# Attention and a gated MLP in one kernel: the bias load of the last 64 rows of two heads, as one load or as one per head

## The chip, the cores and the metric

One core of a Trainium2 chip runs the whole program. The metric is the device time of one execution, in microseconds (us). The kernel before takes 776.21 us, the median of 3 runs (774.19 to 776.37).

## The reference

What is computed, cut to what matters here. There are 4 batches, 8 heads, 576 positions and 64 columns per head. The bias depends on head and positions alone, so it is the same for every batch.

```
scores = scale * q @ k.T                        # per batch and head, 576 x 576
x      = log1p(|i - j|) / log1p(max(i, 1))
bias   = relu(x * w1 + b1) @ w2                 # 576 x 576 x 8 heads
attn   = softmax(scores + bias)
y      = attn @ v                               # 2304 tokens x 512
h      = y @ w_in                               # 512 -> 2048
out    = (max(h, 0) + alpha * min(h, 0)) @ w_out
```

## The kernel before

The bias is computed once. Every `bias_tile` makes it for 16 rows and all heads and writes it to a scratch tensor in HBM (L495); the scratch has three blocks of 256, 256 and 64 rows, each laid out row, head, column. So one row of one head is 576 floats, 2304 bytes in one piece, and the next row of the same head lies 8 heads further on.

The attention is cut into units, one for each batch, half of the heads (`hf`), pair of heads in it (`pr`) and range of rows (`rng`). A unit with `rng` 0 has rows 0 to 255, in two groups of 128 rows. A unit with `rng` 1 has rows 256 to 575: two groups of 128 rows, and then a last group of 64 rows in which the two heads of the pair share one tile, head 0 in partitions 0 to 63 and head 1 in partitions 64 to 127. There are 32 units, 16 of them with `rng` 1, so 16 such last groups.

For each group of a unit:

- SyncE (SP) issues the load of the bias into tile `fg`. A group of 128 rows has one load of 576 KB (L739), in which each partition gets two neighbouring heads, 4608 bytes in one piece. The last group has one load of 288 KB (L751), 128 rows of 2304 bytes.
- TensorE (PE) computes the scores in PSUM (L585 in float32 for the first batch, L586 in float16 parts for the others).
- VectorE (DVE) adds bias and scores and takes the row maximum in one instruction (L765), over `fg` in place.
- ScalarE (ACT) takes the exponential (L768); the sums are turned into a factor (L771, L773, L775).
- Then the rows are normalised and transposed. In most units GpSimd (POOL) scales (L790), PE transposes (L799), and ACT or DVE copies the result out of PSUM (L809, L810). In the units of batch 1 half 1, batch 2 and batch 3 half 1, POOL or ACT writes a float16 part into a tile `a` (L780, L781), DVE writes the remainder (L783), and SP issues DMA transposes from `a` to `at` (L786).
- PE multiplies with v (L828, or L820 in the units with DMA transposes), and ACT and DVE write the result into `x`, the MLP's input (L846, L848).

The MLP runs over 9 chunks of 256 tokens. PE multiplies x with w_in (L895) and the gated result with w_out (L916); ACT (L876, L901, L902, L908) and DVE (L904, L908, L909) do the rest, and SP stores the output (L884). Chunks of the MLP are placed between the units of the attention, so that PE has something to do while a softmax runs.

The order on each engine is made before the program runs, by `Planner.plan`: it simulates the engines with estimated durations and gives each engine the ready operation of lowest key. A plain DMA is an operation of SP that costs 475 ns there, and its landing is estimated from its bytes alone (290 bytes per ns in one shared stream, and 1900 ns more). An operation that lists a tile as written waits for the earlier ones on that tile or on the same part of it; `after` chains the bias loads in the order in which the units are written, and `keep` asks for so many more free tiles. All the engines' instructions run in the order that the plan gives them; SP, too, issues its DMAs strictly one after the other, and each DMA is signalled by one of eight semaphores in turn.

Of the kernel before, what the change touches and what calls it, by code (L numbers as in the profile page):

```python
# [16 lines left out]
B, H, S, D = 4, 8, 576, 64  # L17
HID, DM, DFF = 32, 512, 2048
NT = B * S
P = 128  # L20
# [259 lines left out]
def attention_then_moe(ctx: ExitStack, tc, q, k, v, w1, b1, w2, w_in, w_out, alpha, cst, out):  # L280
# [16 lines left out]
    def halves(ps):  # L297

        return ps.rearrange("p (a n) -> p a n", a=2)[:, :, 0:HS]
# [42 lines left out]
    scr = [dp.tile([min(256, S - i), H, S], F32, name=f"scr{i}") for i in range(0, S, 256)]  # L342
# [37 lines left out]
    def DMA(fn, nbytes, key, r=(), w=(), keep=0, act_q=False, after=None, off=None):  # L380
        alts = [("SP", 475, lambda: fn(nc.sync))]
        if act_q:
            alts += [("ACT", 500, lambda: fn(nc.scalar))]
        return pl.op(alts, key, r, w, dma=("c", nbytes), keep=keep, after=after, off=off)
# [74 lines left out]
    scr_tok = [["scr", i] for i in range(5)]  # L459
# [120 lines left out]
    def score(dst, b, hf, pr, hh, lo, n):  # L580

        qt = qkt[b, hf]
        at = slice(64 * hh, 64 * hh + 64)
        if not in_f16(b, hf):
            return [(lambda a, dst=dst: nc.tensor.matmul(dst(a), lhsT=qt.t[at, 0, pr, lo:lo + n], rhs=qt.t[at, 1, pr, HS * a:HS * a + HS], start=True, stop=True))]  # L585
        return [(lambda a, dst=dst, zq=zq, zk=zk, i=i: nc.tensor.matmul(dst(a), lhsT=tr16(qt)[at, 0, pr, zq, lo:lo + n], rhs=tr16(qt)[at, 1, pr, zk, HS * a:HS * a + HS],  # L586
                                                                         start=(i == 0), stop=(i == 2)))
                for i, (zq, zk) in enumerate(((0, 0), (0, 1), (1, 0)))]
# [128 lines left out]
    last = [None]  # L717
# [4 lines left out]
    def unit(b, hf, pr, rng, key):  # L722
# [3 lines left out]
        hp = 4 * hf + 2 * pr  # L726
# [4 lines left out]
        for ti, grp in enumerate(groups):  # L731
            ky = key + 0.01 * ti
            n = 2 if grp else 1
            sl = [Buf(cS) for _ in range(n)]
            if grp:
                L = Buf(c_f2)
                i0 = grp[0][1]
                blk, r = divmod(i0 // P, 2)
                last[0] = DMA(lambda e, blk=blk, r=r, L=L: e.dma_start(out=L.t, in_=scr[blk][P * r:P * r + P, hp:hp + 2, :]),  # L739
                              P * S * 8, ky, [scr_tok[i0 // P]], [L], keep=1, after=last[0], off="kL")  # L740
                ls = [lambda L=L, hh=hh: L.t[:, hh] for hh in range(2)]

                def mm(sl=sl, i0=i0):
                    both = [score(lambda a, hh=hh: halves(sl[hh].t)[:, a], b, hf, pr, hh, i0, P) for hh in range(2)]
                    for a in range(2):
                        for two in zip(*both):
                            for one in two:
                                one(a)
            else:
                L = Buf(c_f)  # L750
                last[0] = DMA(lambda e, L=L: e.dma_start(out=L.t, in_=scr[2][:, hp:hp + 2, :].rearrange("p h j -> h p j")),  # L751
                              P * S * 4, ky, [scr_tok[4]], [L], keep=1, after=last[0], off="kL")
                ls = [lambda L=L: L.t]

                def mm(sl=sl):
                    both = [score(lambda a, hh=hh: halves(sl[0].t)[64 * hh:64 * hh + 64, a], b, hf, pr, hh, 512, 64) for hh in range(2)]
                    for a in range(2):
                        for two in zip(*both):
                            for one in two:
                                one(a)  # L760
# [176 lines left out]
    for j in range(4):  # L937
        unit(0, j // 2, j % 2, 0, j)
    for t in range(16, NBT):
        bias_tile(t, o_("b16", 0.6) + o_("bk", 0.2) * (t - 16))  # L940
    for j in range(4):
        unit(0, j // 2, j % 2, 1, 4 + j)
    for b in range(1, B):
        v_rows(b, 8 * b - 5)
        for hf in range(2):
            qk_turn(b, hf, 8 * b + 4 * hf - 4.5)
        kappas(b, whole, 8 * b - 2)
        n = 8 * b
        for hf in range(2):
            for rng in range(2):  # L950
                for pr_ in range(2):
                    unit(b, hf, pr_, rng, n)
                    n += 1
# [57 lines left out]
```

## Time and profile before

| what | value |
|---|---|
| median of 3 runs | 776.21 us (774.19 to 776.37) |
| profiled execution, its own time | 779.22 us |
| its span, first to last instruction | 777.1 us |
| PE busy | 701.6 us, 90% of the span |
| DVE, ACT, POOL busy | 521.4, 448.3, 118.9 us |
| mean granted TensorE clock | 0.977 |
| DMA traffic | 114.03 MB, 147 GB/s over the span |

The span is what the profiler sees from the first instruction to the last; the profiled execution's own time is 2.1 us longer. An engine counts as busy while it executes, not while its sequencer waits or issues DMAs; so SP, which only issues, has no busy time. In rows of the timeline, the brackets at the end give the idle time of the engine ahead of that row and the instruction that ended it.

### The profile page before, as it was taken

Reading aid. Unit: us, or ns where it says so; the run is one execution under the profiler, and the core shown is the slowest. Engines: PE = TensorE matmul, PEld = TensorE weight load, DVE = VectorE, ACT = ScalarE, POOL = GpSimd, SP = SyncE. Lnnn points to the kernel's source line nnn. Section 1 sums busy time; section 2 is a strip of 40 time slices with the busy share of each in tenths; the row PEclk is TensorE's granted clock in tenths of the full one; section 3 lists DMA queues with packets and bytes.
Section 4 is the critical chain, followed back from the end, with each engine's and each line's share of the span. In section 5 each row is a group of like instructions: output and inputs, shape, how many; then the busy total and the mean of one; then the engine's idle time right before and its main releaser. Section 6 shows DMA issues by size and latency. Waiting matters only on the chain. (4 is left out here: it accounts for less than half of the span.)

```text
span 777.1 us, 14633 instructions
## 1 busy us (share of the span) xinstructions
PE 701.6 (90%) x5425; PEld 434.9 (56%) x5425; DVE 521.4 (67%) x1281; ACT 448.3 (58%) x826; POOL 118.9 (15%) x149
## 2 busy tenths in 40 slices
PE   4878777787999989997999899999999999999997
PEld 2432343355565746664565656566677566666664
DVE  6888978794887867776767667666467566423442
ACT  5879978774665666664645556555476456222221
POOL 0000232221432212121012011112122001000000
PEclk9999988899999999999999999999999999999999
DMA  7999856423449164989799979798226986200000
GB/s 199 243 271 375 306 184 225 155 85 114 108 117 232 55 194 114 184 158 187 166 183 161 155 183 173 140 159 168 95 87 159 140 149 134 29 28 1 13 16 27
DMA packets 180518, 114.03 MB, mean 147 GB/s; under 512 B 157024, under 2 KB 157024, under 8 KB 180448
## 3 DMA queue, kind: packets, MB, share of 16 engines
q1 hardware_dynamic: 178144, 113.11, 62.8%
q8 instruction: 42, 0.69, 0.4%
q10 hardware_dynamic: 2304, 0.01, 0.2%
q14 instruction: 28, 0.23, 0.1%
HBM read 74.16 MB, written 15.34 MB: 115 GB/s over the span
## 5 line engine op out<-in xcount | busy, mean ns | idle before, releaser
L916 PE MATMUL O<-wout,mg 128*128 128x512 f16 x864 | 200.8, 381 | 4.9 <-ACT mg L876 1.1
L895 PE MATMUL H<-x,win 128*128 128x256 f16 x1728 | 201.5, 273 | 1.2 <-ACT mg L902 1.1
L895 PEld LDWEIGHTS <-win 128*128 128x128 f16 x1728 | 167.3, 98 | 34.2 <-issue 7.5
L768 ACT ACTIVATE fg<-fg,st 128x576 f32<-128x576 f32 x144 | 110.4, 768 | 54.0 <-DVE st L765 49.1
L916 PEld LDWEIGHTS <-mg 128*128 128x128 f16 x864 | 81.8, 98 | 99.3 <-issue 9.7
L901 ACT ACTIVATE mg<-H,sm 128x512 f32<-128x512 f32 x72 | 49.4, 687 | 131.9 <-PE H L895 119.8
L904 DVE SCALAR_TENSOR_TENSOR mg<-mg,sm 128x256 f32<-128x256 f32 x144 | 68.6, 505 | 81.9 <-ACT mg L902 81.6
L765 DVE CUSTOM_DVE_ANT_0 fg<-S,fg 128x576 f32<-128x576 f32 x128 | 93.7, 751 | 35.5 <-PE S L586 24.4
L790 POOL TENSOR_SCALAR fg<-fg,st 128x576 f32<-128x576 f32 x72 | 62.6, 882 | 187.7 <-DVE st L775 81.2
L482 PE MATMUL S<-at,w2b 128*32 128x512 f32 (+1 forms) x448 | 63.3, 457 | 22.3 <-DVE at L470 11.0
L783 DVE SCALAR_TENSOR_TENSOR a<-fg,st,a 128x576 f16<-128x576 f32 x72 | 60.3, 842 | 22.4 <-POOL a L780 12.7
L780 POOL TENSOR_SCALAR a<-fg,st 128x576 f16<-128x576 f32 x40 | 35.4, 886 | 239.8 <-DMA at<-a 75.1
L473 ACT ACTIVATE at<-cst 128x576 f32<-128x576 f32 x89 | 63.7, 765 | 5.8 <-DVE cst L433 5.8
L586 PE MATMUL S<-qk 64*128 64x288 f16 (+1 forms) x654 | 52.0, 287 | 8.2 <-DVE st L765 7.4
L482 PEld LDWEIGHTS S<-at,w2b 128*32 128x32 f32 x448 | 22.8, 116 | 62.3 <-issue 18.1
L799 PE MATMUL S<-cst,fg 128*128 128x128 f32 x290 | 42.4, 285 | 12.2 <-POOL fg L790 8.9
L909 DVE TENSOR_TENSOR mg<-mg 128x512 f16<-128x512 f32 x68 | 47.2, 695 | 3.6 <-ACT mg L908 2.1
L902 ACT ACTIVATE mg<-H,sm 128x512 f32<-128x512 f32 x72 | 49.0, 681 | 0.8 <-DVE mg L909 0.7
L586 PEld LDWEIGHTS <-qk 64*128 64x128 f16 (+1 forms) x720 | 32.1, 97 | 31.0 <-issue 25.4
L828 PE MATMUL A<-at,five 128*64 128x320 f32 (+3 forms) x320 | 46.9, 430 | 0.6 <-DVE at L810 0.6
L799 PEld LDWEIGHTS S<-cst,fg 128*128 128x128 f32 x290 | 32.8, 144 | 20.9 <-POOL fg L790 11.9
L820 PE MATMUL A<-at,five 128*64 128x256 f16 (+3 forms) x480 | 35.5, 295 | 4.4 <-DMA at<-a 4.4
(136 smaller groups left out, 788.2 us busy)
## 6 DMA issues: line engine op xcount, KB each, us to landing
fg<-scr SPq DMA_DIRECT2D x64, 576.0 KB, 4.0
scr<-fg SPq DMA_DIRECT2D x36, 288.0 KB, 6.2
mg<-in_moe_w_in_dram SPq DMA_DIRECT2D x13, 512.0 KB, 6.1
mg<-in_moe_w_out_dram SPq DMA_DIRECT2D x12, 512.0 KB, 3.5
fg<-scr SPq DMA_DIRECT2D x16, 288.0 KB
out_dram<-mg SPq DMA_DIRECT2D x18, 256.0 KB, 2.5
five<-in_q_dram SPq DMA_DIRECT2D x32, 128.0 KB, 5.2
five<-in_k_dram SPq DMA_DIRECT2D x32, 128.0 KB, 4.4
```

The lines of the kernel that those rows point to most:

```text
L473: nc.scalar.activation(hb.t, R[:, lo:lo + S], AF.Relu, bias=PSI[:, g:g + 1], scale=1.0)
L482: nc.tensor.matmul(ps.t[32 * gl:32 * gl + 32, c:n], lhsT=w2b, rhs=hs[gl].t[:, c:n], start=True, stop=True)
L586: return [(lambda a, dst=dst, zq=zq, zk=zk, i=i: nc.tensor.matmul(dst(a), lhsT=tr16(qt)[at, 0, pr, zq, lo:lo + n], rhs=tr16(qt)[at, 1, pr, ...
L765: V(lambda x=x, sl=sl, st=st, ls=ls: nc.vector.tensor_tensor_reduce(out=in_halves(ls[x]()), in0=halves(sl[x].t), in1=in_halves(ls[x]()), s ...
L768: A(lambda x=x, st=st, ls=ls: nc.scalar.activation(ls[x](), ls[x](), AF.Exp, bias=st.t[:, x:x + 1], scale=-1.0, accum_out=st.t[:, 2 + x:3 ...
L783: V(lambda x=x, rec=rec, ls=ls, a16=a16: nc.vector.scalar_tensor_tensor(a16.t[:, 640:640 + S], ls[x](), rec(), a16.t[:, 0:S], op0=ALU.mult ...
L790: pl.op([("POOL", 850, lambda x=x, st=st, ls=ls: nc.gpsimd.tensor_scalar(ls[x](), ls[x](), st.t[:, 6 + x:7 + x], 1.0, op0=ALU.mult, op1=AL ...
L799: nc.tensor.transpose(t5()[:, c], ls[x]()[:, lo:lo + P], EYE)
L895: nc.tensor.matmul(hb.t[:, f, :], lhsT=win[:, fp, zw, kb, P * f:P * f + P], rhs=x[:, zx, kb, :], start=(n == 0), stop=(n == 11))
L901: A(lambda: nc.scalar.activation(g.t, hv(), AF.Relu, scale=sp), 700, ky, [hb, t_sig], [g])
L904: V(lambda f=f: nc.vector.scalar_tensor_tensor(g.t[:, 256 * f:256 * f + 256], nn.t[:, 256 * f:256 * f + 256], nal[:, 2 * fp + f:2 * fp + f ...
L916: nc.tensor.matmul(ob.t[:, t, :], lhsT=gg.t[:, zg, f, P * t:P * t + P], rhs=wout[:, fp, zw, f, :], start=(first and f == 0 and (zg, zw) == ...
```

## The change

The last group's bias load is issued as two loads, each for one head: 64 rows of 2304 bytes from the scratch into 64 partitions. The second one asks for no spare tile beyond its own (`keep`), since its tile is already taken. The plan counts half the bytes for each. Both stay in the chain of the bias loads. Nothing that is computed changes, and no other line is touched; all lines behind it have a number that is higher by one.

```diff
             else:
                 L = Buf(c_f)
-                last[0] = DMA(lambda e, L=L: e.dma_start(out=L.t, in_=scr[2][:, hp:hp + 2, :].rearrange("p h j -> h p j")),
-                              P * S * 4, ky, [scr_tok[4]], [L], keep=1, after=last[0], off="kL")
+                for hh in range(2):
+                    last[0] = DMA(lambda e, L=L, hh=hh: e.dma_start(out=L.t[64 * hh:64 * hh + 64], in_=scr[2][:, hp + hh, :]),
+                                  64 * S * 4, ky, [scr_tok[4]], [(L, ("b", hh))], keep=1 - hh, after=last[0], off="kL")
                 ls = [lambda L=L: L.t]
```

On DVE, ACT and POOL the order of the instructions is the same as before. On SP each of the 16 loads is replaced by two. The first of them, in the first batch (`scr_106` is the scratch block of the last 64 rows, `scr_105` that of rows 256 to 511, `fg` the bias tiles), before:

```order
L495 DMA scr_106<-fg 128x576
L751 DMA fg<-scr_106 128x1x576
L739 DMA fg<-scr_105 128x1152 x2
L751 DMA fg<-scr_106 128x1x576
L739 DMA fg<-scr_105 128x1152 x2
```

and with the change, on SP in the same place:

```order
L495 DMA scr_106<-fg 128x576
L752 DMA fg<-scr_106 64x576 x2
L739 DMA fg<-scr_105 128x1152 x2
L752 DMA fg<-scr_106 64x576 x2
L739 DMA fg<-scr_105 128x1152 x2
```

Everything around the loads keeps its place here, and each large load behind stands one issue later.

In 15 of the 16 places the two loads stand together. In one, in batch 2 among the DMA transposes (`at<-a`), SP's order before is

```order
L739 DMA fg<-scr_105 128x1152
L751 DMA fg<-scr_106 128x1x576
L786 DMA_TRANSPOSE at_83<-a_86 128x10x128
L786 DMA_TRANSPOSE at_83<-a_87 128x10x128
L507 DMA five_78<-in_q_dram 128x4x64 x4
```

and with the change

```order
L739 DMA fg<-scr_105 128x1152
L752 DMA fg<-scr_106 64x576
L787 DMA_TRANSPOSE at_83<-a_86 128x10x128
L752 DMA fg<-scr_106 64x576
L787 DMA_TRANSPOSE at_83<-a_87 128x10x128
L507 DMA five_78<-in_q_dram 128x4x64 x4
```

The second half of the load now stands behind one transpose. On PE one instruction moves, early in the first batch: the transposition of a weight's maxima (L452). Before:

```order
L585 MATMUL S_65<-qk_80 128x288
L585 MATMUL O_63<-qk_80 64x288 x4
L799 MATMUL S_64<-cst,fg 128x128 x5
L452 MATMUL A_66<-cst,sm 2x128
L799 MATMUL S_65<-cst,fg 128x128 x5
```

and with the change

```order
L585 MATMUL S_65<-qk_80 128x288
L452 MATMUL A_66<-cst,sm 2x128
L585 MATMUL O_63<-qk_80 64x288 x4
L800 MATMUL S_64<-cst,fg 128x128 x5
L800 MATMUL S_65<-cst,fg 128x128 x5
```

It stands ahead of four score products and one transposition that it stood behind.

## Rows read from the trace of the kernel before

**Rows 1.** Stretch of the attention: from:to, length, busy PE, PEld, DVE, ACT, POOL, PE clock, DMA share, GB/s.

```profile
172.20:670.00 497.80, 470.70 (x3813) 306.12 (x3811) 342.72 (x874) 285.62 (x565) 89.33 (x114) 0.99 0.73 146
```

**Rows 2.** Timeline of SP and DVE, the first two loads and the instructions that read them.

```profile
170.08 0.32 SPq L495 DMA_DIRECT2D scr<-fg  x1
172.22 0.61 SPq L751 DMA_DIRECT2D fg<-scr  x1
...
173.83 0.52 SPq L751 DMA_DIRECT2D fg<-scr  x1
...
181.96 0.76 DVE L765 CUSTOM_DVE_ANT_0 fg<-O,fg 128x576 f32<-128x576 f32 x1 [4.28 <-DMA fg<-scr]
...
191.25 0.76 DVE L765 CUSTOM_DVE_ANT_0 fg<-O,fg 128x576 f32<-128x576 f32 x1 [5.74 <-DMA fg<-scr]
```

**Rows 3.** DMA issues, KB each and median us to landing (the page's part 6).

```profile
fg<-scr SPq DMA_DIRECT2D x64, 576.0 KB, 4.0
```

**Rows 4.** Short stretches, columns as in rows 1.

```profile
171.08:172.08 1.00, 1.00 (x11) 0.73 (x10) 1.00 (x3) 0.07 (x1) 0.00 (x0) 1.00 0.60 230
...
179.00:181.00 2.00, 2.00 (x18) 1.55 (x17) 0.00 (x0) 0.95 (x4) 0.00 (x0) 1.00 0.13 51
...
442.00:444.00 2.00, 2.00 (x20) 1.80 (x19) 0.69 (x4) 0.87 (x2) 0.00 (x0) 1.00 0.13 51
```

**Rows 5.** Timeline of PE, where it idled for a bias add or for what follows one.

```profile
182.78 1.19 PE L585 MATMUL O<-qk 64*64 64x288 f32 x8 [1.37 <-DVE st L765]
184.93 0.99 PE L799 MATMUL S<-cst,fg 128*128 128x128 f32 x5 [0.96 <-POOL fg L790]
192.99 1.85 PE L585 MATMUL S<-qk 64*128 64x288 f32 x8 [2.38 <-DVE at L810]
196.71 0.74 PE L799 MATMUL S<-cst,fg 128*128 128x128 f32 x5 [0.84 <-DVE st L765]
...
285.29 1.49 PE L799 MATMUL S<-cst,fg 128*128 128x128 f32 x10 [0.65 <-POOL fg L790]
...
515.27 2.75 PE L916 MATMUL O<-wout,mg 128*128 128x512 f16 x12 [0.84 <-DVE st L765]
```

**Rows 6.** Timeline of PE, where it idled behind DMA transposes.

```profile
359.67 1.59 PE L586 MATMUL S<-qk 64*128 64x288 f16 x11 [4.63 <-DVE st L765]
...
447.57 3.09 PE L820 MATMUL A<-at,five 128*64 128x256 f16 x30 [2.94 <-DMA at<-a]
494.76 0.91 PE L586 MATMUL S<-qk 64*128 64x288 f16 x12 [1.49 <-DVE st L765]
...
622.38 1.95 PE L820 MATMUL A<-at,five 128*64 128x256 f16 x30 [1.45 <-DMA at<-a]
```

**Rows 7.** The transposes' line: ns min/median/max of an issue, first and last start; landing.

```profile
L786 SPq DMA_TRANSPOSE at<-a x80: 1206/1364/5372, 299.4 to 662.2; - x80
...
DMA to landing us min/median/max: 3.0/3.8/8.5
```

**Rows 8.** Timeline of SP and ACT behind two of the loads.

```profile
342.64 0.54 SPq L751 DMA_DIRECT2D fg<-scr  x1
...
348.69 7.86 SPq L786 DMA_TRANSPOSE at<-a  x3
...
357.31 0.77 ACT L781 ACTIVATE a<-fg,st 128x576 f16<-128x576 f32 x1 [5.16 <-DMA at<-a]
...
434.34 0.57 SPq L751 DMA_DIRECT2D fg<-scr  x1
...
436.60 8.53 SPq L786 DMA_TRANSPOSE at<-a  x2
```

**Rows 9.** Stretches in which the granted clock was low, columns as in rows 1.

```profile
185.30:188.70 3.40, 3.40 (x19) 2.76 (x18) 0.20 (x2) 1.19 (x4) 0.19 (x1) 0.50 0.29 68
359.40:362.80 3.40, 3.13 (x15) 1.37 (x15) 2.61 (x12) 2.54 (x7) 0.00 (x0) 0.51 1.06 184
448.10:451.50 3.40, 3.40 (x27) 1.87 (x24) 1.84 (x7) 2.58 (x8) 0.75 (x1) 0.50 0.92 291
```

**Rows 10.** SP's issues by line: ns min/median/max, first and last start us.

```profile
L739 SPq DMA_DIRECT2D fg<-scr x64: 319/384/1532, 66.5 to 632.8; - x64
...
L751 SPq DMA_DIRECT2D fg<-scr x16: 503/533/612, 172.2 to 633.5; - x16
```

## The prediction

> **What bounds the kernel now.** I read the busy times by stage first, then the idle times of PE, then what stood ahead of each. In the stretch from 172 to 670 us, in which all 16 of the changed loads lie, PE is busy for 470.70 of 497.80 us [rows 1]; DVE, the next, for 342.72. So PE sets the pace: a load that lands earlier gains only what it takes off PE's 27.10 us of idle time there, and off the stretches with a low clock. Ahead of 172 us and behind 670 us nothing of the change is issued, and the work there stays as it is.
>
> The changed loads are slow. The first is issued at 172.22, and the bias add that reads it starts at 181.96, released by a DMA on `fg`: 9.74 us. The second, issued at 173.83, is read at 191.25, 17.42 us later; DVE had stood for 5.74 us [rows 2]. A load from the same scratch with twice the bytes (L739) lands in 4.0 us in the median [rows 3]. While only such a load is left in flight, the 16 DMA engines together are busy at 0.13, which is two of 16, and move 51 GB/s; this stands at 179 to 181 and again at 442 to 444 us [rows 4]. It isn't the row length of 2304 bytes: the store issued at 170.08 [rows 2] has 128 rows of the same length, and in the second after 171.08 us the engines moved 230 GB/s at a share of 0.60 [rows 4]. What sets the load apart is its access pattern: in the code its source has the two heads as the outermost dimension, of size 2.
>
> The Trainium skill, DMA: Bandwidth & Descriptors, section "Why a DMA increments its semaphore by 16 and not by 1", says that the number of DMA engines is the largest up to 16 that divides the outermost size of both patterns. That would make 2 before and 16 after; the share of 0.13 agrees for before, and no run here shows the 16 yet.
>
> The harm goes two ways. **Directly**, DVE waits for the load, holds its in-order queue, and PE waits for DVE or for what follows it [rows 5]. **Through the queue**, whatever has a share on the two busy DMA engines stands behind the load, the DMA transposes most of all: an issue of one takes 1364 ns in the median and up to 5372, and it lands in 3.8 us in the median and up to 8.5 [rows 7]. After the load at 342.64, three transposes occupy SP from 348.69 for 7.86 us and ACT waits 5.16 us for them; after that at 434.34, two occupy it for 8.53 us [rows 8]. PE then idles [rows 6].
>
> **The change, part by part.** Each half has 64 rows, so it can be spread as the store was; it has 144 KB.
>
> *Landing.* No row shows a load of 64 rows by itself. The upper end is today's 9.74 us [rows 2]; the lower is the transposes' shortest landing, 3.0 us [rows 7]. I take 4 to 5 us: the large load usually issued just ahead lands in 4.0 [rows 3], and the halves' 288 KB at the store's 230 GB/s [rows 4] are 1.3 us.
>
> *Direct waits.* The adds at 181.96 and 191.25 could have begun 4.28 and 5.74 us earlier for all but the load [rows 2], which is 5.46 and 11.68 us after their issues. So a landing at 5 us takes away the first wait entirely; the second load, behind two large ones, has 11.68 less the 4.28 by which DVE is then earlier, 7.40 us. PE's idle times that go with them are 1.37, 0.96, 2.38 and 0.84 us at the first two loads, and 0.65 and 0.84 at two later ones [rows 5]: 7.04 us, and I take all of it.
>
> *Transposes.* PE's idle times are 4.63, 2.94, 1.49 and 1.45 us [rows 6], 10.51 together. Where a transpose lands in 3.8 instead of 8.5 us, it gives back 4.7 of the 5.16 us that ACT waited [rows 7, 8]; so about 0.5 us stays. I leave 0.5 at each of the four places, by choice at the other three: 8.5 us.
>
> *Clock.* In three stretches the granted clock was 0.50 or 0.51, that is the 1.2 GHz level, after PE had idled: 1.37 and 0.96 us ahead of 185.3, 4.63 ahead of 359.67, 2.94 ahead of 447.57 [rows 5, 6, 9]. PE was busy for 3.40 + 3.13 + 3.40 = 9.93 us in them [rows 9]; at 2.4 GHz half would do, so 4.97 us at most. With the idle times gone the low stretches should go, but idle times of other origin remain (27.10 less 17.55), and one could be followed by such a stretch. I take two of three: 3.3 us.
>
> *Costs.* SP issues two loads of some 384 ns each (the time of L739) in place of one of 533 ns [rows 10]: 0.24 us each, 3.8 over 16 places if all lay on the path. Most of it is hidden, since SP issues loads several us ahead; where transposes stand right behind, it delays them. I take 1.0, with 0 and 3.8 as its ends. DVE's add now waits for two landings, but they come in the same order and the later one decides; the cover is that they land together. The load that is split by a transpose (batch 2) puts one transpose's issue, 1.36 us [rows 7], between its halves; with 5 us against 9.7 that stays within the gain. The moved L452 on PE is a single matmul whose input is old there, and costs nothing.
>
> **Sum.** 7.0 + 8.5 + 3.3 - 1.0 = 17.8 us. The profiled execution, 779.22 us, would go to 761.4. It lies 3.0 above the median of the runs; so from 776.21 I forecast **758.4 us**. All of it with no cost would be 7.04 + 10.51 + 4.97 = 22.5; with a quarter of the remaining 9.55 us of idle time besides, which I allow because many instructions stand behind the slow loads, 24.9: 751.3 us.
>
> **Rivals.**
>
> *Only the direct waits go.* The transposes could be slow by themselves, or by the 144 KB and more of other loads around them. For it: there are 80 of them, and SP has less spare time there. Against: the long ones stand behind L751 [rows 8], and the median is 3.8 us. Then 7.04 + 1.70 for the first low stretch - 1.0 = 7.7 us: 768.5.
>
> *No change.* The load is slow not because of the number of engines, but because of its source rows, which lie 8 heads apart; the halves then take as long together. Against: L739 reads at the same distance, with 4608 bytes a row, and lands in 4.0 us [rows 3]. Then only hidden issues are added: about 776.5.
>
> *Slower.* The two halves use the same few engines one after the other, so the landing of the second stays at 9.7 us, and each issue costs SP 0.24 us more ahead of the large loads and the transposes that stand behind it in order: 776.2 + 3.8 = 780.0. It decides if the DMA share behind a pair of loads stays at 0.13 as in rows 4. The Trainium skill speaks for it: DMA: Bandwidth & Descriptors, section "Rules for kernel authors", advises against two transfers to disjoint halves of the partitions, since they share the same engines, and for one of 128 partitions. By that rule the time would be about 780.0 here. The trace's 0.13 speaks against its premise, as one load of 128 partitions does not use all the engines.
>
> **How the numbers follow.** The forecast, with its own range of 751 to 764, has 0.75; direct waits alone 0.15; no change 0.05; slower 0.05. From 751 to 768.5 leaves out the last two and little more. A measurement of this kernel can tell about 0.3%, 2.3 us, from no change. The first two cases are both faster: 0.90; same 0.05; slower 0.05.
>
> **What would show it.** Right: the time from a pair's issue to its bias add drops below 6 us or the wait of DVE for `fg` vanishes; no stretch of some us at a DMA share of 0.13 and 51 GB/s; no issue of a transpose of 5 us; PE's idle time from 172 us to the end of the attention falls from 27 to about 10 us, with its busy time some 3 us lower. Wrong: the share of 0.13 remains (slower or no change), or transposes still land in 8 us with the loads early (direct waits alone), or PE's idle time comes back in front of other instructions.

## The result, and the profile after

The changed kernel takes 746.75 us (median; 744.54 to 747.89) against 776.0 us: a ratio of 0.9624, with a 95% interval of 0.9596 to 0.9652. It is 29.3 us faster, where 17.8 were forecast and 751.0 us was the lower end of the range.

In these stretches the profiled execution is cut at the issue of the first changed load, before (at 172.22 us) and after (at 164.58). Columns as in rows 1.

```profile
0.00:172.22 172.22, 128.43 (x914) 62.43 (x916) 141.62 (x332) 135.93 (x218) 29.56 (x35) 0.93 0.72 230
172.22:777.10 604.88, 573.16 (x4513) 372.46 (x4509) 379.81 (x950) 312.35 (x609) 89.33 (x114) 0.99 0.61 123
```

```profile
0.00:164.58 164.58, 121.78 (x914) 59.85 (x916) 141.52 (x332) 135.64 (x218) 29.49 (x35) 0.97 0.76 240
164.58:742.80 578.22, 565.72 (x4513) 370.07 (x4509) 379.74 (x950) 311.40 (x609) 87.69 (x114) 1.00 0.58 129
```

From the first changed load to the end the kernel is 26.66 us shorter: PE's idle time (length less busy) falls from 31.72 to 12.50, that is by 19.22, and its busy time for the same 4513 matmuls by 7.44. Ahead of that load both execute the same 914 matmuls, yet after is 7.64 us shorter there, with PE's granted clock at 0.97 instead of 0.93. The change has no instruction in that part; see the last two experiments.

The first loads and the adds that read them, in the timeline of after, answer to [rows 2]:

```profile
164.58 1.13 SPq L752 DMA_DIRECT2D fg<-scr  x2
...
166.86 1.23 SPq L752 DMA_DIRECT2D fg<-scr  x2
...
169.97 0.74 DVE L766 CUSTOM_DVE_ANT_0 fg<-O,fg 128x576 f32<-128x576 f32 x1
...
175.26 0.75 DVE L766 CUSTOM_DVE_ANT_0 fg<-O,fg 128x576 f32<-128x576 f32 x1
```

The adds start 5.39 and 8.40 us after the issues, where it was 9.74 and 17.42, and have no idle time ahead of them. The halves' issues and landings, and the page's line of the large loads, in after:

```profile
L752 SPq DMA_DIRECT2D fg<-scr x32: 450/535/1383, 164.6 to 600.5; - x32
...
DMA to landing us min/median/max: 2.8/4.6/6.9
```

```profile
fg<-scr SPq DMA_DIRECT2D x64, 576.0 KB, 4.6
```

The large loads land later than before, 4.6 us after the issue in the median where it was 4.0 [rows 3]. The engines' rate behind the loads, against the 0.13 and 51 GB/s of [rows 4] (the share adds up the packets' times, so it can pass 1.00):

```profile
168.90:169.90 1.00, 0.77 (x7) 0.31 (x4) 1.00 (x3) 1.00 (x3) 0.00 (x0) 1.00 1.04 429
...
415.00:417.00 2.00, 2.00 (x30) 1.10 (x28) 0.93 (x3) 0.98 (x4) 0.00 (x0) 1.00 1.12 269
```

The transposes' line of after, against [rows 7]:

```profile
L787 SPq DMA_TRANSPOSE at<-a x80: 1206/1348/2885, 282.9 to 627.5; - x80
...
DMA to landing us min/median/max: 2.9/3.5/6.8
```

The longest issue of a transpose falls from 5372 to 2885 ns. And where PE waited 4.63 us at 359.67 [rows 6], ACT no longer waits for a transpose:

```profile
335.30 0.78 ACT L782 ACTIVATE a<-fg,st 128x576 f16<-128x576 f32 x1
...
339.44 0.89 PE L586 MATMUL S<-qk 64*128 64x288 f16 x11 [1.13 <-DVE st L766]
```

PE's longest waits from 164 to 640 us, in after's list of waits (who waited for whom: us in total, times, longest):

```profile
PE S L586 <- DVE st L766: 2.4, 2, 1.3
PE H L896 <- ACT mg L903: 1.1, 4, 0.5
PE O L917 <- ACT at L810: 0.8, 1, 0.8
```

No wait for a DMA is left among them.

### The profile page after: what moved, and what is told of

The parts are those of the page before. It is cut to its first block, busy times and chain, and to the rows that moved or that the text cites. A ratio compares the mean times of both kernels' runs of the same rounds, so it can differ in the third digit from the quotient of the medians.

```text
span 742.8 us, 14670 instructions
## 1 busy us (share of the span) xinstructions
PE 687.5 (93%) x5425; PEld 429.9 (58%) x5425; DVE 521.3 (70%) x1281; ACT 447.0 (60%) x826; POOL 117.2 (16%) x149
## 3 DMA queue, kind: packets, MB, share of 16 engines
q10 hardware_dynamic: 2304, 0.01, 0.2%
## 4 chain that ended last, share of the span: by engine, by line
PE 62%; DMA 1%; DVE 1%; ACT 1%; issue 0%; SPq 0%; ACTq 0%; DVEq 0%
PE O L917 23%; PE H L896 22%; PE S L586 5%; PE A L821 4%; PE A L829 2%; PE S L800 2%; PE S L560 2%; DMA fg<-scr 1%; DVE fg L766 1%; PE O L800 0%; PE O L586 0%; ACT mg L877 0%; DMA out_dram<-mg 0%; PE A L455 0%; ACT fg L769 0%
## 5 line engine op out<-in xcount | busy, mean ns | idle before, releaser
L766 DVE CUSTOM_DVE_ANT_0 fg<-S,fg 128x576 f32<-128x576 f32 x128 | 93.7, 751 | 33.6 <-PE S L586 29.3
L781 POOL TENSOR_SCALAR a<-fg,st 128x576 f16<-128x576 f32 x40 | 33.5, 838 | 221.9 <-DMA at<-a 51.1
L586 PEld LDWEIGHTS <-qk 64*128 64x128 f16 (+1 forms) x720 | 31.8, 97 | 25.9 <-issue 20.7
L829 PE MATMUL A<-at,five 128*64 128x320 f32 (+3 forms) x320 | 44.9, 415 | 0.6 <-DVE at L811 0.6
```

Of the source, the lines that this page charges most:

```text
L766: V(lambda x=x, sl=sl, st=st, ls=ls: nc.vector.tensor_tensor_reduce(out=in_halves(ls[x]()), in0=halves(sl[x].t), in1=in_halves(ls[x]()), s ...
```

## The experiments

The theory: an access pattern with two heads outermost puts the old load on two of the 16 DMA engines, where it takes long and holds up all that shares them; the halves use all. The rivals: that the moved instructions gained, that smaller transfers gain by themselves, or that two loads are needed. In e1 to e4, e6, e7, e9 and e10 one operation of the plan issues all the parts, so that the order of all instructions of PE, DVE, ACT and POOL is that of before, and on SP only the load is replaced.

**e1: the change without its moves.**

```diff
-last[0] = DMA(lambda e, L=L: e.dma_start(out=L.t, in_=scr[2][:, hp:hp + 2, :].rearrange("p h j -> h p j")),
-              P * S * 4, ky, [scr_tok[4]], [L], keep=1, after=last[0], off="kL")
+def both_halves(e, L=L):
+    for hh in range(2):
+        e.dma_start(out=L.t[64 * hh:64 * hh + 64], in_=scr[2][:, hp + hh, :])
+last[0] = DMA(both_halves, P * S * 4, ky, [scr_tok[4]], [L], keep=1, after=last[0], off="kL")
```

> Both halves are issued inside one operation of the plan, so that the order on PE, DVE, ACT and POOL is that of the kernel before and on SP only the load is doubled. Theory 1 (the old load runs on two of 16 DMA engines, the halves on all): the gain stays, 0.957 to 0.968 of before, 743 to 751 us. Rival (the moved matmul, the moved transpose or the halved bytes in the plan made the gain): within 0.5% of before, 772 to 780 us.

746.71 us, a ratio of 0.9603 (0.9549 to 0.9656): the whole gain. The moved matmul and the moved transpose have no part in it.

**e2: two parts by columns, both with two heads outermost.** The edit, against e1:

```diff
-    for hh in range(2):
-        e.dma_start(out=L.t[64 * hh:64 * hh + 64], in_=scr[2][:, hp + hh, :])
+    for c in range(2):
+        e.dma_start(out=L.t[:, HS * c:HS * c + HS],
+                    in_=scr[2][:, hp:hp + 2, HS * c:HS * c + HS].rearrange("p h j -> h p j"))
```

> The load is cut in two by columns: each part has both heads as its outermost dimension and half of the bytes. Theory 1: both parts stay on two engines one after the other, the DMA share behind a pair stays at 0.13, and the bias add starts 9 to 12 us after the first issue: 774 to 786 us. Rival (two smaller transfers are faster by themselves, whatever their pattern): most of the gain, 745 to 755 us.

776.1 us, 0.9976 (0.9948 to 1.0004). Two smaller loads gain nothing by themselves: the first add starts 9.55 us after the issue, within the 9 to 12 expected, behind a wait of 4.09 us. The rate behind them, a stretch of e2:

```profile
178.00:180.00 2.00, 1.03 (x11) 0.86 (x10) 1.60 (x5) 2.00 (x5) 1.57 (x2) 1.00 0.13 47
```

**e3, e4, e9 and e10: four loads of one head each, with row counts chosen for their divisors.** The edit, against e1 and with 62, 56, 57 and 61 in turn:

```diff
     for hh in range(2):
-        e.dma_start(out=L.t[64 * hh:64 * hh + 64], in_=scr[2][:, hp + hh, :])
+        for lo, hi in ((0, 62), (62, 64)):
+            e.dma_start(out=L.t[64 * hh + lo:64 * hh + hi], in_=scr[2][lo:hi, hp + hh, :])
```

> Each head's 64 rows come as 62 and 2 rows, four loads in place of one. Theory 1, in the form that the number of engines follows from the common factor of rows and 16: 62 rows use two engines, so the landing stays at 9 us or more and the time is 772 to 790 us. Rival (it is only the dimension of two heads that is slow, any list of single rows is spread): 745 to 756 us, the gain less 32 more issues of some 0.4 us on SP. The Trainium skill, DMA: Bandwidth & Descriptors, section on why a DMA increments its semaphore by 16, gives two engines for 62 rows.

> The same four loads with 56 and 8 rows. Theory 1: 14 and 8 engines (or all), so the landing is 4 to 6 us and the gain stays but for 32 more issues: 744 to 758 us. Rival (four issues in place of one are what would make the 62 and 2 rows slow): as slow as with 62 and 2 rows, within 1%.

> Each head's 64 rows come as 57 and 7 rows, with the order of before. If the number of engines is the largest up to 16 that divides the rows, the 57 rows go by three. By the 51 GB/s that two engines moved, three move 76: 263 KB take 3.4 us, against 5.5 us for 62 rows on two. So the landing is some 2 us shorter than with 62 rows and still longer than the 4.5 us of the halves: 752 to 768 us, between the two. Rival (all row counts that are not a multiple of 8 are equally slow): 773 us or more.

> 61 and 3 rows: 61 has no divisor up to 16 but one, so one engine moves 281 KB at some 25.5 GB/s, 11 us, with its share of the large loads 12.5, and the landing is 14 to 15 us. Each load then blocks the queue some 5 us longer than before: slower than before by at least as much as the halves gained, 800 to 835 us. Rival (rows that don't divide fall back to two engines or to the spread of the rest): 772 to 785 us.

Of each the first load and its add in the timeline, and for e3, e9 and e10 a stretch in which little but such loads was in flight. First e3, 62 and 2 rows:

```profile
170.28 1.26 SPq L754 DMA_DIRECT2D fg<-scr  x4
...
180.77 0.76 DVE L769 CUSTOM_DVE_ANT_0 fg<-O,fg 128x576 f32<-128x576 f32 x1 [5.03 <-DMA fg<-scr]
```

```profile
178.00:180.00 2.00, 1.47 (x11) 0.71 (x9) 0.00 (x0) 0.02 (x1) 0.00 (x0) 1.00 0.13 50
```

e4, 56 and 8 rows:

```profile
167.06 1.40 SPq L754 DMA_DIRECT2D fg<-scr  x4
...
172.45 0.75 DVE L769 CUSTOM_DVE_ANT_0 fg<-O,fg 128x576 f32<-128x576 f32 x1
```

e9, 57 and 7 rows:

```profile
169.63 1.29 SPq L754 DMA_DIRECT2D fg<-scr  x4
...
177.29 0.76 DVE L769 CUSTOM_DVE_ANT_0 fg<-O,fg 128x576 f32<-128x576 f32 x1 [2.19 <-DMA fg<-scr]
```

```profile
177.00:178.00 1.00, 1.00 (x11) 0.71 (x10) 0.71 (x3) 0.38 (x2) 0.00 (x0) 1.00 0.19 76
```

e10, 61 and 3 rows, and its part from the first of these loads to the end:

```profile
164.39 4.29 SPq L754 DMA_DIRECT2D fg<-scr  x4
...
179.43 0.76 DVE L769 CUSTOM_DVE_ANT_0 fg<-O,fg 128x576 f32<-128x576 f32 x1 [9.56 <-DMA fg<-scr]
```

```profile
190.00:192.00 2.00, 0.00 (x0) 0.00 (x0) 0.00 (x0) 0.00 (x0) 0.00 (x0) 0.81 0.07 25
```

```profile
164.39:858.00 693.61, 599.05 (x4513) 386.42 (x4509) 378.93 (x950) 312.19 (x609) 89.56 (x114) 0.93 0.56 107
```

| rows of the large part | largest divisor up to 16 | semaphore updates per load | share, GB/s | issue to add, us | time, us | ratio to before |
|---|---|---|---|---|---|---|
| 61 | 1 | 2 | 0.07, 25 | 15.04 | 861.04 | 1.1065 (1.1019 to 1.1112) |
| 62 | 2 | 3 | 0.13, 50 | 10.49 | 779.84 | 1.0029 (0.999 to 1.0068) |
| 57 | 3 | 4 | 0.19, 76 | 7.66 | 755.18 | 0.9713 (0.9682 to 0.9743) |
| 56 | 14 | 15 | no such stretch | 5.39, no wait | 748.75 | 0.9606 (0.9572 to 0.964) |

The shares are one, two and three sixteenths, and the rate grows by 25 GB/s an engine. The traces also hold every update of the semaphore that a load signals. Counted from a load's issue to the next issue on the same semaphore, they are 2, 3 and 4 for these, and 3, 4, 8 and 9 for the small parts of 2, 3, 7 and 8 rows: the divisor and one more. The 56 rows have 15, which makes 14 engines. The old load has 3, as have both parts of e2; the halves have 16, as have the large loads (L739), which is taken as all 16 engines. So the count of engines goes with the divisor, whatever the pattern of heads, and the time goes with the count. That is the rule of the Trainium skill, DMA: Bandwidth & Descriptors, section "Why a DMA increments its semaphore by 16 and not by 1"; the runs agree, by shares for one, two and three engines and by updates for 14 and 16 too. The number of loads matters little: with the same four, 56 rows keep the gain and 62 lose it. e10 lands about when it was expected to (14 to 15 us) but is 26 us slower than the end of its range: PE's idle time behind the first load is 94.6 us, three times that of before, and its busy time 25.9 us above before's, at a granted clock of 0.93.

**e5: one load, from a scratch whose last block is stored head by head** (four stores go into that block; the other stores keep their form).

```diff
-scr = [dp.tile([min(256, S - i), H, S], F32, name=f"scr{i}") for i in range(0, S, 256)]
+scr = [dp.tile([256, H, S], F32, name=f"scr{i}") for i in range(0, 512, 256)]
+scr += [dp.tile([H, 64, S], F32, name="scr512")]
...
-e.dma_start(out=scr[blk][r0:r0 + 16].rearrange("r h j -> (r h) j"), in_=ev.t)
+e.dma_start(out=scr[2][:, r0:r0 + 16, :].rearrange("h r j -> r h j"), in_=ev.t)
...
-e.dma_start(out=L.t, in_=scr[2][:, hp:hp + 2, :].rearrange("p h j -> h p j"))
+e.dma_start(out=L.t, in_=scr[2][hp:hp + 2].rearrange("h p j -> (h p) j"))
```

> One load again, of 128 rows, but the scratch of the last 64 rows is stored head by head, so that the load's source is one block of 128 rows; the four stores into it go by 16 rows of 8 heads. Theory 1: a single load of 128 partitions is spread over all engines and lands in 4 us or less, at least the whole gain, 740 to 750 us, with 16 fewer issues on SP than two halves. Rival (the gain needs two loads): 770 us or more.

747.87 us, 0.9633 (0.9603 to 0.9662): the gain doesn't need two loads. One load whose source is 128 rows in a single dimension does the same. Its semaphore has 16 updates per load, and it lands later than the 4 us that were expected at most, 4.8 in the median:

```profile
DMA to landing us min/median/max: 2.8/4.8/6.5
```

The issues that it saves on SP are worth nothing that can be measured. The Trainium skill, DMA: Bandwidth & Descriptors, section "Rules for kernel authors", prefers one transfer of 128 partitions to two halves; the runs agree that two halves are no better than one such transfer that is spread, and differ for one that is not.

**e6 and e7: only half of the units.** The halves are issued in the units without DMA transposes (e6: `if not by_dma(b, hf)`), or only in those with (e7: `if by_dma(b, hf)`); the others keep the old load.

> The load is halved only in the eight units whose probabilities PE transposes; the eight units with DMA transposes keep the old load. The order is that of before. Theory: the direct waits at the first loads go with it, PE's idle time falls by some 7 us and the low stretch of the clock at 185 us goes: 8 to 12 us gained, 764 to 769 us. Rival (the transposes' queue carries all of it): within 4 us of before.

> The converse: halved only in the eight units with DMA transposes. Theory: the idle times behind transposes and their low stretches go, 10.5 us of idle and 3.3 us of clock: 12 to 18 us gained, 758 to 764 us; with the other experiment the gains add up to that of the whole change within 3 us. Rival (the queue of the transposes stays slow by itself): within 5 us of before.

767.12 us, 0.9887 (0.9843 to 0.9931), and 758.16 us, 0.976 (0.972 to 0.9799). The part from the first of these loads to the end, in e6 and then e7:

```profile
167.12:763.90 596.78, 570.22 (x4513) 371.20 (x4509) 380.13 (x950) 312.14 (x609) 89.29 (x114) 0.99 0.62 125
```

```profile
167.03:755.40 588.37, 569.66 (x4513) 372.46 (x4509) 379.98 (x950) 312.21 (x609) 88.47 (x114) 0.99 0.56 127
```

Against before's 604.88 and 573.16, e6 takes 8.10 us off this part: 5.16 of PE's idle time (31.72 to 26.56) and 2.94 of its busy time. e7 takes off 16.51: 13.01 (31.72 to 18.71) and 3.50. Together 24.6 of the 26.7. Part of what lacks is lost at the first loads in e7: there the 2.38 us of idle time of [rows 5] has grown to 3.97 while the 0.84 us behind it has gone, and the low stretch of the clock lasts 6.8 us where it was 3.4 [rows 9]. Two thirds of the gain come from the units with transposes. The transposes' line and landing, in e6 and then e7:

```profile
L792 SPq DMA_TRANSPOSE at<-a x80: 1205/1368/5460, 285.3 to 648.6; - x80
...
DMA to landing us min/median/max: 3.0/3.5/9.2
```

```profile
L792 SPq DMA_TRANSPOSE at<-a x80: 1206/1350/3248, 295.9 to 640.5; - x80
...
DMA to landing us min/median/max: 3.0/3.6/6.7
```

So the long issues and landings of transposes go with the old loads among them. With one engine (e10) the longest issue is 8687 ns, with two (e3) 5437, with three (e9) 4365, with 14 (e4) 2800.

**e8, e11 and e12: both kernels profiled again.**

> The kernel before, profiled once more. Question: are the 172 us ahead of the first changed load always as long? If the low stretches of the clock there come by chance, this profile shows another sum of them than 23.9 us and the first changed load is issued between 163 and 173 us; if they belong to the kernel, it is issued at 172 again.

> The kernel before, a third profile, for the part ahead of the first changed load, which took 172 us in two profiles of it and 165 to 170 in eight others. If the low clock there comes by chance, it is 163 to 172 again with another sum of low stretches; if it belongs to this kernel, 172.

> The changed kernel, a second profile. From the first changed load to the end it should take 577 to 579 us again, with PE idle for 7.5 us up to 700 us and no low stretch of the clock there; the part ahead of the first changed load took 164.6 us and should be 164 to 172.

Before twice more, and after once more, up to the first changed load and from there:

```profile
0.00:171.96 171.96, 128.31 (x914) 62.38 (x916) 141.44 (x332) 135.93 (x218) 29.56 (x35) 0.93 0.73 230
171.96:778.00 606.04, 573.07 (x4513) 372.32 (x4509) 379.46 (x950) 312.24 (x609) 89.49 (x114) 0.99 0.62 123
```

```profile
0.00:169.38 169.38, 127.07 (x914) 62.01 (x916) 141.53 (x332) 135.81 (x218) 29.48 (x35) 0.94 0.73 233
169.38:775.30 605.92, 574.35 (x4513) 372.94 (x4509) 380.02 (x950) 312.14 (x609) 90.44 (x114) 0.99 0.61 123
```

```profile
0.00:171.07 171.07, 124.94 (x914) 61.68 (x916) 141.40 (x332) 135.71 (x218) 29.48 (x35) 0.91 0.73 231
171.07:749.20 578.13, 565.71 (x4513) 369.92 (x4509) 380.44 (x950) 311.41 (x609) 87.52 (x114) 1.00 0.58 129
```

From the first changed load on, after repeats itself to 0.1 us (578.22 and 578.13) and before to 1.2 (604.88 to 606.04). Ahead of it after took 164.58 and then 171.07 us, before 172.22, 171.96 (e8) and 169.38 (e11), and e2 and e10, slow as they are, 166.50 and 164.39. e8 had its first load at 172 again, which by its expectation speaks for the kernel; e11 had it earlier. That part varies from one execution to the next, with the granted clock between 0.91 and 0.97, and doesn't go with the slow load. With its long first part the second profiled execution of after took 751.24 us, more than any of the four runs of the result (744.54 to 747.89).

## Why the prediction was wrong, point by point

The mechanism held. Two terms of the sum were too small, the one for the transposes and the one for the clock, and the cost was too high.

- **The bound, the two engines and the two ways of harm** were read rightly. The share of 0.13 meant two engines: e3, e9 and e10 show shares of two, three and one. The way through the queue shows in e6 and e7.
- **Landing:** 4 to 5 us was taken, and the halves' median is 4.6; the first add starts 5.39 us after the issue and waits for nothing, the second 8.40 us after, where 7.40 was allowed, without a wait.
- **Direct waits:** 7.0 us. Of its six idle times five, 6.2 us, lie in the units without transposes; with the 1.7 us of the first low stretch that makes 7.9, and e6 took off 8.10. Right in sum, though split otherwise: 5.16 of idle and 2.94 of busy time.
- **Transposes:** a term that was mis-sized. It stood at 8.5 us, with the 0.84 us at 515.27 [rows 5] some 9.3; e7 took off 13.01 us of idle time. Two steps were wrong. At each of four places 0.5 us was left standing, by analogy with one of them; in after only one of them keeps an idle time, the 1.13 us at 339.44, so 0.9 us too much was left. And shorter idle times were put down to "other origin". PE's list of waits in e6, where the old loads still stand among the transposes, has them:

```profile
PE O L922 <- DVE mg L915: 1.0, 3, 0.3
PE O L922 <- ACT mg L882: 1.0, 1, 1.0
...
PE S L560 <- DVE st L771: 0.7, 1, 0.7
```

In e7's list the first of them is down to 0.2 us in one wait, and the other two are missing: they went with the loads among the transposes.

- **Clock:** the other mis-sized term. 3.3 us was taken, and 4.97 called the most; PE's busy time fell by 7.44 us, and the granted clock reads 1.00 for the part behind the first load. The fear that idle times of other origin would bring a low stretch did not come true: all three low stretches [rows 9] went where two were taken, which is worth up to 4.97 us. At least 2.5 us of the busy time are not the clock's, and the prediction has no term for them. Busy time also fell where the clock was granted in full before and after. In the next lines the same 50 matmuls, just behind the first low stretch, are shown before and after, and then the same 143 further on:

```profile
188.81:199.10 10.29, 7.07 (x50) 5.07 (x48) 7.58 (x21) 5.32 (x11) 3.42 (x4) 1.00 0.22 64
410.95:433.26 22.31, 20.51 (x143) 12.70 (x142) 15.57 (x33) 11.59 (x20) 4.05 (x5) 1.00 1.02 186
```

```profile
177.16:183.48 6.32, 6.32 (x50) 4.78 (x47) 5.77 (x15) 4.45 (x9) 3.42 (x4) 1.00 0.44 111
389.26:409.04 19.78, 19.78 (x143) 12.76 (x143) 15.89 (x33) 11.48 (x20) 2.45 (x4) 1.00 0.90 170
```

Busy time is 0.75 and 0.73 us less. Both stretches hold idle times in before and none in after. One matmul in the second of them, in before and then in after:

```profile
425.88 0.39 PE L916 MATMUL O<-wout,mg 128*128 128x512 f16 x1 [0.53 <-DVE mg L908]
```

```profile
401.64 0.71 PE L896 MATMUL H<-x,win 128*128 128x256 f16 x5
402.18 2.54 PE L917 MATMUL O<-wout,mg 128*128 128x512 f16 x11
```

Behind an idle time it counts with its whole 0.39 us; in after, where it is the first of the 11, it starts 0.17 us before the row ahead of it ends, and those 0.17 us count once. So an idle time that went took some busy time with it. These two stretches have 1.48 us of it; where the rest of the 2.5 us lies is not shown.

- **Costs:** 1.0 us was taken off, from issues of 384 ns each. The halves' issues took 535 in the median, so two in place of one of 533 cost SP 0.54 us, 8.6 over 16 places; none of it is seen in the time. e4 issues 32 loads more than e1, and its part from the first load to the end is 577.74 us against e1's 578.10:

```profile
167.06:744.80 577.74, 565.62 (x4513) 370.01 (x4509) 379.76 (x950) 311.35 (x609) 89.29 (x114) 1.00 0.56 129
```

```profile
167.10:745.20 578.10, 565.62 (x4513) 369.93 (x4509) 379.96 (x950) 311.38 (x609) 87.16 (x114) 1.00 0.58 129
```

So the added issues cost nothing that can be seen.

- **The sum and the range:** 17.8 us stood against 26.66 in the two profiles: 19.22 of idle time where 15.5 was taken, 7.44 of busy time where 3.3 was, and no cost where 1.0 was. The range's lower end held 24.9 us: 17.55 of listed and 2.4 of other idle time, 4.97 of clock. The idle time stayed within that, the busy time did not. With the mean of three profiles of before (605.61 us from the first changed load on) and two of after (578.18) the gain there is 27.4 us, a ratio of 0.9647 to 776.0 and inside the measured interval. The medians' 29.3 us have some 2 us more. The part ahead of the first load varies by more than that between executions; whether chance is all of it stays open.
- **The rivals:** direct waits alone is refuted by e7, no change and slower by the result; e2 is the case in which the slower rival's premise (the same few engines) holds, and it is no slower than before, so its 3.8 us for issues was too much as well.

## What to carry to other kernels

A DMA can have 128 rows and still run on two engines, if one side's outermost dimension is 2: look for stretches at a DMA share of 1/16 or 2/16, and reorder the access pattern or the scratch so that the outermost dimension is the rows, and their number has a large divisor up to 16 (64, 128 and 56 rows gained here). Price such a load by what queues behind it on the same engines, not by its own wait: here the units with transposes gave twice what the direct waits did. And when a stall holds an in-order engine, count the small idle times behind it too, and the busy time that goes with them.

## What was not expected of the hardware

Row counts as close as 61 and 62 of the same data differ by 81 us in this kernel (861.04 and 779.84), since the first runs on one DMA engine and the second on two. The rate is 25 GB/s an engine for rows of 2304 bytes: 25, 50 and 76 GB/s for one, two and three engines.

The part of the program that the change doesn't touch took from 164.39 to 172.22 us in the profiles named here, for the same 914 matmuls, with the granted clock between 0.91 and 0.97. A difference of some us between two single profiles of this kernel says nothing until it is located.
